# Pacing a weight preparation by the steps of the product beside it, and exchanging two operations between VectorE and GpSimd

## The chip, the cores and the metric

The kernel runs on one core of one Trainium2 chip. The metric is the device time of one execution in microseconds; lower is better. Engines are named as in the profile: PE is TensorE, DVE is VectorE, ACT is ScalarE, POOL is GpSimd and SP is SyncE, whose queue issues nearly all DMAs here.

## The reference

Three stages in float32, one after the other, on 4 x 576 = 2304 tokens of 512 columns:

```
local = softmax(causal(q k^T / 8)) v                 # 4 batches, 8 heads, 64 columns each
mem   = (phi(q) M_prev) / (phi(q) z_prev + 1e-6)     # phi(x) = elu(x) + 1
x     = sigmoid(beta) mem + (1 - sigmoid(beta)) local
r     = relu(x w_in)                                 # 2304 x 2048
y     = (s r^2 + b) w_out                            # 2304 x 512
out   = (sigmoid(y w_gate) * (y w_val)) w_out2       # inner width 1536
```

The weights arrive as 64-bit floats. s and b are one number each.

## The kernel before, in words

Every matrix product is made from split numbers: an operand is rounded to a high part, the low part is the difference, and three products (high x high, low x high, high x low) are summed in PSUM. So every operand costs a rounding on ScalarE and a subtraction on VectorE or GpSimd.

The program runs in overlapping stages. In the attention stage, 16 jobs (a batch and two heads) give x, batch by batch; `s_hi` and `s_lo` (lines 886 to 894) split x into its parts, in two windows of 256 and 320 tokens for each batch. h = x w_in is made in 128 blocks (`h_mm`, line 310) of 12 matmuls each, 16 column blocks for each of 8 windows; ScalarE applies the relu and r goes to DRAM (`h_store`). When attention is over, y is made: 6 windows of 384 tokens times 16 column blocks are 96 steps (`plan_step`, line 1013). One step loads 128 x 384 numbers of r (SyncE), squares them (ScalarE), makes s r^2 + b in place (`scale`, line 1027), rounds them to gh (`g_hi`, ScalarE), makes the low part gl (`g_lo`, line 1038) and multiplies both with w_out in 12 matmuls (`y_mm`). Each buffer is one of a few: 4 for r, 3 each for gh and gl.

Each 64-bit weight tile of 128 x 512 numbers is turned into float32 by integer operations (`weight_parts`): `scaled` on ScalarE, two VectorE passes in `rest` (lines 250 and 253), a third in `joined` (line 259); a split weight then gets its high part (ScalarE) and low part (GpSimd, line 268). w_in has 16 tiles, w_out 16, w_out2 12. w_gate and w_val together are 12 blocks n of two tiles each (`plan_blocks`, line 1129): each block gets four sums on VectorE (line 1159), and the seven 256-column pieces are stored in DRAM (weight_scratch). These raw tiles share 4 buffers with those of w_out.

The last stage takes y in three pairs of windows. For each pair, the products m of y's combinations with the seven pieces are made in 12 groups (gate and value of one column block f in turn, `plan_group`); their sums on VectorE give, after a sigmoid and a multiplication on GpSimd, the rows f and f + 6 of p, which has 12 rows. `plan_out` (line 1361) then makes each of six output tiles of 128 tokens in three thirds of four rows of p each, with w_out2.

The order of the work is not that of the program text. A planner (`Plan.order`) is given tasks with an engine, an estimated duration, a due time ("urgency"), buffers to hold and tasks to follow, simulates the engines, and lets each free engine take the ready task with the lowest due time. Its result is the fixed order of instructions on every engine. `late` is the time that it adds before a task counts as finished (60 ns, 250 for TensorE, 1900 or 2500 for DMAs). The due times come from the table `TUNE`: w_gate and w_val's is `gv` + n x `gvs`, y's is `y` + 10 for each step, h's is `h` + `hs` for each block.

Of the kernel before, what the change touches and what calls it, by code (L numbers as in the profile page):

```python
# [8 lines left out]
F32 = mybir.dt.float32  # L9
# [21 lines left out]
}  # L31
ENG = {"split": "POOL"}
RR = 4
RAW2 = 4
RING = 5
SETS = 3


class Plan:
# [25 lines left out]
    def order(self):  # L65
# [34 lines left out]
        while len(out) < len(tasks):  # L100
            for eng in clock:
                if clock[eng] > now:
                    continue
                for n in ready.get(eng, []):
                    t = tasks[n]
                    if not can(t):
                        continue
                    ready[eng].remove(n)
                    for tag, x in t[6]:
                        free[tag] -= 1  # L110
                        if tag in heads:
                            heads[tag] += 1
                    self.start[n] = now
                    out.append(n)
                    clock[eng] = now + t[1]
                    end = now + t[1] + t[7]
                    if t[8]:
                        dma = max(dma, now + t[1]) + t[8] / RATE
                        end = max(end, dma + t[7])
                    heapq.heappush(events, (end, n))  # L120
                    heapq.heappush(events, (clock[eng], -1))
                    break
            assert events, [
                (tasks[n][3], tasks[n][6]) for q in ready.values() for n in q
            ]
            now = max(now, events[0][0])
            changed = set()
            while events and events[0][0] <= now:
                _, n = heapq.heappop(events)
                if n < 0:  # L130
                    continue
                for x in tasks[n][5]:
                    touches[x] -= 1
                    if not touches[x] and x in self.made:
                        free[self.made[x][0]] += 1
# [12 lines left out]
def attention_moe_kernel(  # L148
# [58 lines left out]

    def load_consts():

        nc.sync.dma_start(gt, beta.partition_broadcast(P))  # L210
        nc.sync.dma_start(sb_s, s_in.partition_broadcast(P))
        nc.sync.dma_start(sb_b, b_in.partition_broadcast(P))
# [211 lines left out]
    def stack_lo(t, ds):  # L424
# [10 lines left out]
        "raw2": RAW2, "f2": FB, "w2": 16, "rr": RR, "gh": 3, "gl": 3, "yacc": 2,  # L435
# [495 lines left out]
    def plan_weight(pool, src, name, cols, u, key, tag, done=None, ins=(), late=False):  # L931

        raw, fl = ("raw2", "f2") if late else ("raw", "f")
        box, load, scaled, rest, joined, high, low = weight_parts(
            pool, src, name, cols, Late("stage") if late else stage
        )
        add(
            "SP", 450, load, u + AT["lw"], reads=ins,
            new=[(raw, ("raw", key))] + ([(tag, key)] if tag else []), late=1900, size=5e5,
        )  # L940
        add("ACT", 670, scaled, u, reads=[("raw", key)], new=[(fl, ("f", key))])
        add("DVE", 1500, rest, u, writes=[("raw", key)])
        add("DVE", 850, joined, u, reads=[("f", key)], writes=[("raw", key)])
        if tag:
            add("ACT", 660, high, u, reads=[("raw", key)], writes=[key])
            add("POOL", 1360, lambda: done(low()), u, reads=[("raw", key)], writes=[key])
        return box
# [65 lines left out]
    def plan_step(step):  # L1013
# [12 lines left out]

        def scale():
            r = r_sb[step]
            nc.vector.tensor_scalar(  # L1029
                out=r, in0=r, scalar1=sb_s, scalar2=sb_b, op0=ALU.mult, op1=ALU.add  # L1030
            )

        def g_hi():
            gh = Y["gp"].tile([P, WT], F32R, tag="gh", name=f"gh{wi}_{f}", bufs=3)
            nc.scalar.copy(gh, r_sb[step])  # L1035
            gs[step] = [gh]

        def g_lo():
            gl = Y["gp"].tile([P, WT], F32R, tag="gl", name=f"gl{wi}_{f}", bufs=3)
            nc.gpsimd.tensor_tensor(  # L1040
                out=gl, in0=r_sb.pop(step), in1=gs[step][0].bitcast(F32), op=ALU.subtract
            )
            gs[step].append(gl)
# [22 lines left out]
            size=n * 512,  # L1066
        )
        add("ACT", act(n), square, v, writes=[rk])
        add("DVE", 450, scale, v, writes=[rk])
        add("ACT", act(n), g_hi, v, reads=[rk], new=[("gh", gk)])  # L1070
        add("POOL", 130 + 2.4 * n, g_lo, v, reads=[rk, gk], new=[("gl", ("gl", step))])
        new = [("yacc", ("ya", wi))] if f == 0 else []
        add(
            "PE", 12 * mm(n), y_mm, u,
# [54 lines left out]
    def plan_blocks(n):  # L1129
# [5 lines left out]
        raws = [  # L1135
            plan_weight(
                None, src[:, (f + i * HF) * P : (f + i * HF + 1) * P], f"gv{n}_{i}", True, u + i,
                keys2[i], None, ins=["bar1"], late=True,
            )
            for i in range(2)  # L1140
        ]
# [22 lines left out]
        add("DVE", 900, lambda: sums(0), u, reads=[k0, k1, ("wm", n)], writes=[("wm", n, 1)])  # L1164
        add("DVE", 900, lambda: sums(1), u, reads=[k0, k1, ("wm", n)], writes=[("wm", n, 1)])
# [89 lines left out]
    def plan_group(pi, g, f, u):  # L1255
# [67 lines left out]
        for i, xs in enumerate(PAIRS):  # L1323
            m, k = len(xs) * 2 * P, ("ws", z, i)
            add("ACT", 130 + 0.9 * m, lambda i=i: hi(i), v + i, reads=[("wf", z)], new=[("ws", k)])
            add(
                LOS[i], 150 + 1.05 * m if LOS[i] == "DVE" else 130 + 2.4 * m, lambda i=i: lo(i),
                v + i, reads=[("wf", z)], writes=[k],
            )
        k = lambda o: ("c", z, o)  # L1330
# [18 lines left out]
        for o in (0, 3, 2, 1):  # L1349
# [8 lines left out]
                writes=[("pp", pi, f + HF * OF[o][0], OF[o][1])], new=new,  # L1358
            )

    def plan_out(pi, tt, u):

        h, r = divmod(tt, WT // P)
# [2 lines left out]

        def hi(i):
            t = Z["ps", z, i] = Y["ws"].tile([P, 2, 512], F32R, tag="ws", name=f"ps{pi}_{tt}_{i}")
            nc.scalar.copy(t[:, 0].rearrange("p (f n) -> p f n", n=P), src(i))  # L1369

        def src(i):
            return Z["p", pi][:, 4 * i : 4 * i + 4, h, r * P : (r + 1) * P]

        def lo(i):
            t = Z["ps", z, i]
            nc.vector.tensor_tensor(  # L1376
                out=t[:, 1].rearrange("p (f n) -> p f n", n=P), in0=src(i),
                in1=t[:, 0].bitcast(F32).rearrange("p (f n) -> p f n", n=P), op=ALU.subtract,
            )

        def out_mm(i):
            if i == 0:
                Z["zo", z] = Y["ps_zo"].tile([P, DM], F32, tag="zo", name=f"o{pi}_{tt}")
            for k in range(4):
                f = 4 * i + k
                for a, x in ((0, 0), (1, 0), (0, 1)):
                    nc.tensor.matmul(  # L1387
                        Z["zo", z], Z["ps", z, i][:, a, k * P : (k + 1) * P],
                        w_out2_sb[f][:, x].rearrange("p c f -> p (c f)"),
                        start=(f == 0 and a == x == 0), stop=(f == NF2 - 1 and x == 1),  # L1390
                    )

        def evict():
# [5 lines left out]

        v = u - AT["pl"]  # L1400
        for i in range(NF2 // 4):
            ins = [("p", pi)] + [("pp", pi, f, h) for f in range(4 * i, 4 * i + 4)]
            k = ("ps", z, i)
            add("ACT", act(512), lambda i=i: hi(i), v + i, reads=ins, new=[("ws", k)])
            add("DVE", dve(512), lambda i=i: lo(i), v + i, reads=ins, writes=[k])
            add(
                "PE", 12 * mm(512), lambda i=i: out_mm(i), u + i,
                reads=[k, "bar3b"] + [("w3", f) for f in range(4 * i, 4 * i + 4)],
                writes=[("zo", z)] if i else [], new=[] if i else [("zo", ("zo", z))], late=250,
            )  # L1410
        add("DVE" if tt % 2 else "ACT", act(512), evict, u, reads=[("zo", z)], new=[("raw", ("os", z))])
# [111 lines left out]
```

## Time and profile before

| what | value |
|---|---|
| median of 3 runs | 1136.14 us (1135.06 to 1143.1) |
| profiled execution | 1142.42 us, its span 1140.6 us |
| mean granted TensorE clock | 0.975 |
| busy | PE 1056.0, DVE 786.0, ACT 647.3, POOL 619.2 us |
| DMA | 145.93 MB, mean 128 GB/s |
| chain that ended last | PE 71%, DVE 15%, DMA 4%, issue 3%, POOL 3%, ACT 3% |

The span is the profiled part of one execution; the time beside it has the start and end around it. "Busy" of an engine counts the time in which it works on an instruction, and for a matmul also some of the time in which it waits inside. The chain is followed back from the last instruction to whatever released each step.

### The profile page before, as it was taken

The numbers are of one execution on the slowest core, as the hardware profiler recorded it, in microseconds if no ns is written. First come the engines' busy times: TensorE is split into PE (matmuls) and PEld (weight loads), VectorE is DVE, ScalarE is ACT, GpSimd is POOL, SyncE is SP. The second block draws the span as 40 slices with busy tenths as digits, with TensorE's granted clock in tenths as the row PEclk, the third lists the DMA queues.
The fourth block names the chain that finished last, engine by engine and source line by source line (L and its number), as shares of the span: only waits on it lengthen the run. The fifth ranks groups of instructions, "written<-read, shape, count | busy, mean of one in ns | idle before, by whom it ended". The sixth has DMA issues, their size and how long they took to land.

```text
span 1140.6 us, 18761 instructions
## 1 busy us (share of the span) xinstructions
PE 1056.0 (93%) x6496; PEld 986.6 (86%) x6496; DVE 786.0 (69%) x1426; ACT 647.3 (57%) x1407; POOL 619.2 (54%) x598
## 2 busy tenths in 40 slices
PE   4776999999999989988789999999799998999998
PEld 3665999899999989988688999998689997899986
DVE  5999888777677527868999433999826667166631
ACT  4877777777777655545656544555425553245421
POOL 5657566744454335733665653999615775157710
PEclk9989899999999999988899999999999999999999
DMA  5333453333232157649588634545114330043100
GB/s 129 76 78 100 120 158 119 85 94 94 83 95 66 59 185 207 197 139 346 184 250 289 218 112 133 205 156 193 59 44 146 130 129 10 37 138 130 66 19 37
DMA packets 135598, 145.93 MB, mean 128 GB/s; under 512 B 68176, under 2 KB 123472, under 8 KB 135504
## 3 DMA queue, kind: packets, MB, share of 16 engines
q1 hardware_dynamic: 135504, 144.74, 40.5%
q8 instruction: 51, 0.84, 0.3%
q14 instruction: 43, 0.35, 0.1%
HBM read 106.96 MB, written 37.75 MB: 127 GB/s over the span
## 4 chain that ended last, share of the span: by engine, by line
PE 71%; DVE 15%; DMA 4%; issue 3%; POOL 3%; ACT 3%; SPq 0%; ACTq 0%; DVEq 0%; POOLq 0%
PE m L1291 19%; PE h L316 15%; PE o L1387 13%; PE y L1054 11%; PE sc L623 3%; PE acc L803 2%; PE acc L804 2%; DMA rr<-relu_scratch 1%; DVE wm L1159 1%; PE pt_B L750 1%; DVE rr L1029 1%; PE sc L649 1%; PE ft L413 1%; POOL p L1313 1%; DVE yt L1190 1%
## 5 line engine op out<-in xcount | busy, mean ns | idle before, releaser
L1291 PE MATMUL m<-yt,ws 128*128 128x384 f32 x1512 | 266.9, 336 | 6.5 <-POOL ws L1275 3.9
L1291 PEld LDWEIGHTS m<-yt,ws 128*128 128x128 f32 x1512 | 263.6, 189 | 9.1 <-POOL ws L1275 4.8
L316 PE MATMUL h<-x,w_in 128*128 128x256 f32 (+1 forms) x1536 | 233.6, 305 | 6.9 <-ACT r L326 6.9
L316 PEld LDWEIGHTS h<-x,w_in 128*128 128x128 f32 x1536 | 214.3, 194 | 13.1 <-ACT r L326 8.2
L1303 DVE TENSOR_TENSOR set<-m,set 128x384 f32<-128x384 f32 x252 | 134.2, 553 | 57.4 <-PE m L1291 55.3
L1275 POOL TENSOR_TENSOR ws<-wf,ws 128x512 fp32r<-128x512 f32 (+1 forms) x108 | 123.8, 1165 | 90.5 <-ACT ws L1267 90.4
L1054 PE MATMUL y<-gh,w_out 128*128 128x384 f32 x768 | 155.9, 344 | 17.8 <-ACT gh L1035 16.4
L1040 POOL TENSOR_TENSOR gl<-rr,gh 128x384 fp32r<-128x384 f32 x96 | 111.2, 1169 | 112.2 <-ACT gh L1035 83.9
L1387 PE MATMUL o<-w_out,ps 128*128 128x512 f32 x648 | 155.6, 401 | 8.8 <-DVE ps L1376 8.8
L1387 PEld LDWEIGHTS o<-w_out,ps 128*128 128x128 f32 x648 | 123.6, 191 | 39.7 <-DVE ps L1376 10.0
L1054 PEld LDWEIGHTS y<-gh,w_out 128*128 128x128 f32 x768 | 137.6, 193 | 22.4 <-ACT gh L1035 18.8
L1267 ACT CAST ws<-wf 128x512 fp32r<-128x512 f32 (+1 forms) x144 | 81.1, 568 | 94.2 <-PE m L1291 66.7
L1029 DVE TENSOR_SCALAR rr<-rr,sb_s,sb_b 128x384 f32<-128x384 f32 x96 | 62.5, 663 | 71.5 <-ACT rr L1025 69.2
L1313 POOL TENSOR_TENSOR p<-set,set 128x384 f32<-128x384 f32 x72 | 85.2, 1206 | 45.4 <-DVE set L1303 45.4
L681 POOL TENSOR_SCALAR P<-P,rs 128x384 f32<-128x384 f32 (+3 forms) x144 | 82.9, 599 | 42.0 <-DVE rs L673 24.2
L603 DVE CUSTOM_DVE_ANT_0 P<-sc,mask 128x384 f32<-128x384 f32 (+2 forms) x144 | 70.8, 515 | 34.7 <-PE sc L623 19.2
L665 ACT ACTIVATE P<-P,nm 128x384 f32<-128x384 f32 (+2 forms) x144 | 83.8, 583 | 7.4 <-DVE nm L603 6.7
L1054 PE MATMUL y<-gl,w_out 128*128 128x384 f32 x384 | 84.4, 341 | 1.1 <-POOL gl L1040 1.1
L326 ACT ACTIVATE r<-h 128x320 f32<-128x320 f32 (+1 forms) x128 | 52.2, 409 | 57.3 <-PE h L316 42.2
L1376 DVE TENSOR_TENSOR ps<-p,ps 128x512 fp32r<-128x512 f32 x54 | 47.1, 886 | 50.6 <-ACT ps L1369 50.2
L1025 ACT ACTIVATE rr<-rr 128x384 f32<-128x384 f32 x96 | 49.4, 524 | 50.9 <-DMA rr<-relu_scratch 48.8
L1054 PEld LDWEIGHTS y<-gl,w_out 128*128 128x128 f32 x384 | 69.5, 192 | 2.3 <-POOL gl L1040 2.3
(134 smaller groups left out, 1709.8 us busy)
## 6 DMA issues: line engine op xcount, KB each, us to landing
wf<-weight_scratch SPq DMA_DIRECT2D x36, 896.0 KB, 4.6
rr<-relu_scratch SPq DMA_DIRECT2D x96, 192.0 KB, 3.3
raw_w_out<-in_moe_w_out_dram SPq DMA_DIRECT2D x28, 512.0 KB, 4.3
weight_scratch<-wm SPq DMA_DIRECT2D x12, 896.0 KB, 8.0
relu_scratch<-r SPq DMA_DIRECT2D x32, 320.0 KB, 2.3
raw_w_in<-in_moe_w_in_dram SPq DMA_DIRECT2D x16, 512.0 KB, 4.1
relu_scratch<-r SPq DMA_DIRECT2D x32, 256.0 KB, 2.5
raw_gv<-in_moe_w_gate_dram SPq DMA_DIRECT2D x12, 512.0 KB, 5.6
```

The costliest lines, as they stand in the source:

```text
L316: nc.tensor.matmul(t[:, :n], wt[:, wi, c], x[:, xi, c], start=(m == 0), stop=(m == 3 * NK - 1))
L665: nc.scalar.activation(pr, pr, AF.Exp, bias=T.pop(("nm", j, e, t)), scale=-1.0, accum_out=T["sums", j][:, col : col + 1],)
L681: nc.gpsimd.tensor_scalar(out=pr, in0=pr, scalar1=T["rs", j, part][:, n : n + 1], scalar2=1.0, op0=ALU.mult, op1=ALU.mult,)
L1029: nc.vector.tensor_scalar(out=r, in0=r, scalar1=sb_s, scalar2=sb_b, op0=ALU.mult, op1=ALU.add)
L1040: nc.gpsimd.tensor_tensor(out=gl, in0=r_sb.pop(step), in1=gs[step][0].bitcast(F32), op=ALU.subtract)
L1054: nc.tensor.matmul(accs[wi][d][:, :n], w_out_sb[f][:, x, d], y, start=(f == 0 and x == 0 and y is gh), stop=(f == NF - 1 and y is gl),)
L1267: nc.scalar.copy(t[:, 0, :m], flat(a, m))
L1275: engine[LOS[i]].tensor_tensor(out=t[:, 1, :m], in0=flat(a, m), in1=t[:, 0, :m].bitcast(F32), op=ALU.subtract)
L1291: nc.tensor.matmul(acc, wt[:, a, k : k + P], yt[:, y, c], start=(m == 0), stop=(m == 3 * K2 - 1),)
L1303: nc.vector.tensor_tensor(out=t[:, o], in0=Z["m", z, x], in1=t[:, i], op=ALU.add)
L1313: engine[TIMES[o]].tensor_tensor(out=p[:, f + HF * OF[o][0], OF[o][1]], in0=Z["set", z][:, o], in1=Z["set", zg][:, o], op=ALU.mult,)
L1387: nc.tensor.matmul(Z["zo", z], Z["ps", z, i][:, a, k * P : (k + 1) * P], w_out2_sb[f][:, x].rearrange("p c f -> p (c f)"), start=(f == 0 a ...
```

## The change

The diff, cut to its core:

```diff
-    "pv": 28.5, "split": 117.6, "h": 9920.5, "hs": 56.8, "w": 297.3, "ws": 26.9, "lw": -287.4,
-    "relu": -5000.0, "wo": 31942.3, "wos": 7.3, "gv": 42719.0, "gvs": 58.2, "y": 16976.0,
-    "lead": 25.8, "lr": -189.7, "ys": -139.5, "yss": 39.3, "t0": 63.0, "z": 59940.3, "zw": 311.1,
+    "pv": 34.9, "split": 71.5, "h": 1670.1, "hs": 50.3, "w": 304.5, "ws": 26.9, "lw": -333.7,
+    "relu": -5000.0, "wo": 29200.4, "wos": -2.6, "gv": 39111.5, "gvs": 110.0, "y": 16143.2,
+    "lead": 12.1, "lr": -288.0, "ys": -104.6, "yss": 53.8, "t0": 4.3, "z": 60013.8, "zw": 410.0,
...
-ENG = {"split": "POOL"}
-RR = 4
+ENG = {"split": "DVE"}
+RR = 6
+GG = 4
...
+PACE = 2, 7
@@ class Plan
-                    heapq.heappush(events, (end, n))
-                    heapq.heappush(events, (clock[eng], -1))
+                    heapq.heappush(events, (end, n, 0))
+                    heapq.heappush(events, (clock[eng], n, 1))
...
                 for m in users[n]:
+                    if (tasks[m][0] == tasks[n][0] and not tasks[n][8]) != bool(same):
+                        continue
                     waiting[m] -= 1
@@ load_consts
-        nc.sync.dma_start(gt, beta.partition_broadcast(P))
+        nc.scalar.dma_start(gt, beta.partition_broadcast(P))
...
@@ plan_weight
-        add("DVE", 1500, rest, u, writes=[("raw", key)])
-        add("DVE", 850, joined, u, reads=[("f", key)], writes=[("raw", key)])
+        add("DVE", 1700, rest, u, writes=[("raw", key)])
+        add("DVE", 950, joined, u, reads=[("f", key)], writes=[("raw", key)])
@@ plan_step
         def scale():
-            nc.vector.tensor_scalar(
+            nc.gpsimd.tensor_scalar(
...
         def g_lo():
-            gl = Y["gp"].tile([P, WT], F32R, tag="gl", name=f"gl{wi}_{f}", bufs=3)
-            nc.gpsimd.tensor_tensor(
+            gl = Y["gp"].tile([P, WT], F32R, tag="gl", name=f"gl{wi}_{f}", bufs=GG)
+            nc.vector.tensor_tensor(
...
-        add("DVE", 450, scale, v, writes=[rk])
+        add("POOL", 700, scale, v, writes=[rk])
...
-        add("POOL", 130 + 2.4 * n, g_lo, v, reads=[rk, gk], new=[("gl", ("gl", step))])
+        add("DVE", 650, g_lo, v, reads=[rk, gk], new=[("gl", ("gl", step))])
@@ plan_blocks
-                keys2[i], None, ins=["bar1"], late=True,
+                keys2[i], None, ins=["bar1", ("yc", PACE[0] + PACE[1] * n)], late=True,
...
@@ plan_out
+    THIRD = [list(range(4)), list(range(HF, HF + 4)), [HF - 2, HF - 1, NF2 - 2, NF2 - 1]]
...
-            ins = [("p", pi)] + [("pp", pi, f, h) for f in range(4 * i, 4 * i + 4)]
+            ins = [("p", pi)] + [("pp", pi, f, h) for f in THIRD[i]]
```

In words:

- The raw loads of block n of w_gate and w_val may be planned only after step 2 + 7n of y.
- s r^2 + b moves from VectorE to GpSimd, the low part of g from GpSimd to VectorE. There are 6 buffers for r instead of 4, and 4 each for gh and gl instead of 3. The low part of x (`s_lo`) moves from GpSimd to VectorE.
- In the planner, a task that follows one on its own engine is ready when the engine is free; `late` holds for followers on other engines and for all followers of DMAs.
- The output's thirds are rows 0 to 3, rows 6 to 9, and rows 4, 5, 10, 11 of p, instead of 0 to 3, 4 to 7 and 8 to 11. High and low parts are taken by the same rows.
- The three loads of constants are issued by ScalarE instead of SyncE.
- The due times in `TUNE` have new values (the first, second and last lines of the table are left out above), and some planned durations of VectorE are longer (weights, sums, weight splits).

## Rows read from the trace of the kernel before

**Rows 1.** Busy time by stage: length, then PE, PEld, DVE, ACT, POOL, clock, DMA.
```profile
0.00:120.00 120.00, 81.89 (x506) 65.67 (x507) 98.47 (x234) 81.90 (x194) 75.93 (x97) 0.92 0.39 96
120.00:405.00 285.00, 283.36 (x2276) 270.57 (x2276) 207.66 (x511) 214.16 (x533) 144.42 (x182) 1.00 0.33 95
405.00:500.00 95.00, 87.64 (x573) 85.07 (x571) 60.93 (x77) 51.29 (x109) 53.40 (x37) 0.98 0.67 209
500.00:620.00 120.00, 101.51 (x520) 97.60 (x521) 108.64 (x159) 68.75 (x140) 58.92 (x45) 0.90 0.74 246
620.00:705.00 85.00, 85.00 (x490) 84.76 (x488) 34.23 (x50) 41.31 (x88) 45.15 (x43) 1.00 0.49 154
705.00:810.00 105.00, 93.05 (x506) 89.08 (x505) 99.59 (x136) 59.45 (x114) 91.94 (x69) 0.98 0.51 172
```
**Rows 2.** PE in order of time: start, duration, instructions of y and h.
```profile
450.61 1.55 PE L1054 MATMUL y<-gh,w_out 128*128 128x384 f32 x8
...
452.69 1.91 PE L316 MATMUL h<-x,w_in 128*128 128x320 f32 x12
454.44 1.55 PE L1054 MATMUL y<-gh,w_out 128*128 128x384 f32 x8
```
**Rows 3.** Waits of PE, 405 to 705 us: total, times, longest.
```profile
PE y L1054 <- ACT gh L1035: 16.4, 7, 5.0
PE h L316 <- ACT r L326: 6.9, 3, 3.3
```
**Rows 4.** DVE in order of time: passes with nothing on POOL beside them.
```profile
520.61 0.42 DVE L1159 TENSOR_TENSOR wm<-raw_gv 128x256 f32<-128x256 f32 x1
...
522.08 0.42 DVE L250 TENSOR_SCALAR raw_gv<-raw_gv 128x512 int32<-128x512 int32 x1
522.53 0.69 DVE L253 SCALAR_TENSOR_TENSOR raw_gv<-raw_gv 128x512 int32<-128x512 int32 x1
523.33 0.69 DVE L259 SCALAR_TENSOR_TENSOR raw_gv<-f_gv,raw_gv 128x512 int32<-128x512 int32 x1
...
635.83 0.69 DVE L1275 TENSOR_TENSOR ws<-wf,ws 128x512 fp32r<-128x512 f32 x1 [2.25 <-ACT ws L1267]
```
**Rows 5.** DVE by line, 500 to 620 us; the last row 705 to 810.
```profile
L253 DVE SCALAR_TENSOR_TENSOR raw_gv<-raw_gv 128x512 int32<-128x512 int32 x21 | 20.5, 975 | 0.7
L259 DVE SCALAR_TENSOR_TENSOR raw_gv<-f_gv,raw_gv 128x512 int32<-128x512 int32 x21 | 19.0, 905 | 1.3
L250 DVE TENSOR_SCALAR raw_gv<-raw_gv 128x512 int32<-128x512 int32 x22 | 16.8, 763 | 1.5 <-DMA raw_gv<-in_moe_w_gate_dram 1.5
...
L253 DVE SCALAR_TENSOR_TENSOR raw_w_out<-raw_w_out 128x512 int32<-128x512 int32 x12 | 16.8, 1402 | 0.4
```
**Rows 6.** The two lines that change engine: ns least/median/most, whole span.
```profile
L1029 DVE TENSOR_SCALAR rr<-rr,sb_s,sb_b x96: 467/480/1974, 416.4 to 694.8; 128x384 f32<-128x384 f32 x96
L1040 POOL TENSOR_TENSOR gl<-rr,gh x96: 999/1122/3030, 417.7 to 699.0; 128x384 fp32r<-128x384 f32 x96
```
**Rows 7.** POOL by line and shape, whole span: count, busy us, mean ns.
```profile
L681 POOL TENSOR_SCALAR P<-P,rs 128x384 f32<-128x384 f32 x32 | 19.5, 613 | 42.0 <-DVE rs L673 24.2 <-DVE rs L677 9.0 <-PE acc L807 8.8
```
**Rows 8.** POOL and DVE in order of time at 103 us.
```profile
103.30 2.38 POOL L892 TENSOR_TENSOR x<-XB,x 128x1024 fp32r<-128x1024 f32 x1 [2.00 <-ACT x L888]
103.44 2.79 DVE L253 SCALAR_TENSOR_TENSOR raw_w_in<-raw_w_in 128x512 int32<-128x512 int32 x1
```
**Rows 9.** POOL in order of time: the last split of x.
```profile
409.73 2.96 POOL L892 TENSOR_TENSOR x<-XB,x 128x1280 fp32r<-128x1280 f32 x1 [2.54 <-ACT x L888]
```
**Rows 10.** SP's queue at the start.
```profile
0.74 0.39 SPq L210 DMA_DIRECT2D gt<-in_beta_dram  x1
...
2.12 0.98 SPq L373 DMA_DIRECT2D rawk<-in_k_dram  x2
```
**Rows 11.** PE in order of time where the output starts, with the wait.
```profile
810.48 2.08 PE L1387 MATMUL o<-w_out,ps 128*128 128x512 f32 x4 [4.23 <-DVE ps L1376]
...
952.69 3.66 PE L1387 MATMUL o<-w_out,ps 128*128 128x512 f32 x9 [2.87 <-DVE ps L1376]
```

More of the change, by code (lines that the diff above doesn't have):

```diff
@@ L128, in order @@
             while events and events[0][0] <= now:
[L129 to L135, printed above, removed]
+                _, n, same = heapq.heappop(events)
+                if not same:
+                    for x in tasks[n][5]:
+                        touches[x] -= 1
+                        if not touches[x] and x in self.made:
+                            free[self.made[x][0]] += 1
                 for m in users[n]:
+                    if (tasks[m][0] == tasks[n][0] and not tasks[n][8]) != bool(same):
+                        continue
                     waiting[m] -= 1
@@ L208, in load_consts @@
     def load_consts():
-        nc.sync.dma_start(gt, beta.partition_broadcast(P))
-        nc.sync.dma_start(sb_s, s_in.partition_broadcast(P))
-        nc.sync.dma_start(sb_b, b_in.partition_broadcast(P))
+        nc.scalar.dma_start(gt, beta.partition_broadcast(P))
+        nc.scalar.dma_start(sb_s, s_in.partition_broadcast(P))
+        nc.scalar.dma_start(sb_b, b_in.partition_broadcast(P))
         nc.scalar.activation(gt, gt, AF.Exp, scale=-1.0)
@@ L434, in attention_moe_kernel @@
         "PTC": 1, "XB": 1, "x0": 1, f"x{SPLIT}": 1, "raw": 2, "f": FB, "wt": 16,
-        "raw2": RAW2, "f2": FB, "w2": 16, "rr": RR, "gh": 3, "gl": 3, "yacc": 2,
+        "raw2": RAW2, "f2": FB, "w2": 16, "rr": RR, "gh": GG, "gl": GG, "yacc": 2,
         "yf": 2, "wf": 2, "ws": RING, "set": SETS, "p": 1, "w3": NF2, "z": 4, "zz": 2,
@@ L1033, in g_hi @@
         def g_hi():
-            gh = Y["gp"].tile([P, WT], F32R, tag="gh", name=f"gh{wi}_{f}", bufs=3)
+            gh = Y["gp"].tile([P, WT], F32R, tag="gh", name=f"gh{wi}_{f}", bufs=GG)
             nc.scalar.copy(gh, r_sb[step])
@@ L1163, in plan_blocks @@
         add("ACT", 360, lambda: copies(1), u, reads=[k1, ("wm", n)], writes=[("wm", n, 0)])
-        add("DVE", 900, lambda: sums(0), u, reads=[k0, k1, ("wm", n)], writes=[("wm", n, 1)])
-        add("DVE", 900, lambda: sums(1), u, reads=[k0, k1, ("wm", n)], writes=[("wm", n, 1)])
+        add("DVE", 1100, lambda: sums(0), u, reads=[k0, k1, ("wm", n)], writes=[("wm", n, 1)])
+        add("DVE", 1100, lambda: sums(1), u, reads=[k0, k1, ("wm", n)], writes=[("wm", n, 1)])
         add(
@@ L1326, in plan_group @@
             add(
-                LOS[i], 150 + 1.05 * m if LOS[i] == "DVE" else 130 + 2.4 * m, lambda i=i: lo(i),
+                LOS[i], 150 + 1.75 * m if LOS[i] == "DVE" else 130 + 2.4 * m, lambda i=i: lo(i),
                 v + i, reads=[("wf", z)], writes=[k],
@@ L1368, in hi, with part @@
             t = Z["ps", z, i] = Y["ws"].tile([P, 2, 512], F32R, tag="ws", name=f"ps{pi}_{tt}_{i}")
-            nc.scalar.copy(t[:, 0].rearrange("p (f n) -> p f n", n=P), src(i))
+            nc.scalar.copy(part(t, 0, i), src(i))
+        def part(t, x, i):
+            return t[:, x].rearrange("p (a f n) -> p a f n", a=1 + i // 2, n=P)
         def src(i):
-            return Z["p", pi][:, 4 * i : 4 * i + 4, h, r * P : (r + 1) * P]
+            p = Z["p", pi][:, :, h, r * P : (r + 1) * P]
+            if i < 2:
+                return p[:, i * HF : i * HF + 4].unsqueeze(1)
+            return p.rearrange("p (a f) n -> p a f n", a=2)[:, :, 4:]
         def lo(i):
@@ L1376, in lo @@
             nc.vector.tensor_tensor(
-                out=t[:, 1].rearrange("p (f n) -> p f n", n=P), in0=src(i),
-                in1=t[:, 0].bitcast(F32).rearrange("p (f n) -> p f n", n=P), op=ALU.subtract,
+                out=part(t, 1, i), in0=src(i), in1=part(t, 0, i).bitcast(F32), op=ALU.subtract,
             )
@@ L1384, in out_mm @@
             for k in range(4):
-                f = 4 * i + k
+                f = THIRD[i][k]
                 for a, x in ((0, 0), (1, 0), (0, 1)):
@@ L1389, in out_mm @@
                         w_out2_sb[f][:, x].rearrange("p c f -> p (c f)"),
-                        start=(f == 0 and a == x == 0), stop=(f == NF2 - 1 and x == 1),
+                        start=(i == k == a == x == 0), stop=(i == 2 and k == 3 and x == 1),
                     )
@@ L1407, in plan_out @@
                 "PE", 12 * mm(512), lambda i=i: out_mm(i), u + i,
-                reads=[k, "bar3b"] + [("w3", f) for f in range(4 * i, 4 * i + 4)],
+                reads=[k, "bar3b"] + [("w3", f) for f in THIRD[i]],
                 writes=[("zo", z)] if i else [], new=[] if i else [("zo", ("zo", z))], late=250,
```

6 rows, old and new, of the table TUNE are left out of this document.

## Prediction

> **What bounds the kernel now.** I read the busy time by stage first [rows 1]. From 120 to 405 us TensorE is busy 283.4 of 285 us; nothing on another engine can shorten that stage. Before 120 us it has 38 us idle, and VectorE is the full engine there (98.5 of 120). From 405 to 705 us the 16 remaining blocks of h for the last batch, all of y and the preparation of w_out, w_gate and w_val run together. In its middle, 500 to 620, VectorE is busy 108.6 of 120 us and TensorE's granted clock falls to a mean of 0.90; in the last 85 us TensorE is busy all the time and VectorE only 34.2. The work is the same in kind and badly spread.
>
> How much is lost in these 300 us? The three stages hold 1583 matmuls [rows 1], 1152 of them y's (96 steps of 12). The timeline gives a step of y as 452.69 - 450.61 = 2.08 us and a block of h on 320 columns as 454.44 - 452.69 = 1.75 us [rows 2]. So y needs 96 x 2.08 = 200 us. The other 431 matmuls are h on 320 columns (0.146 us each), h on 256 (scaled, 0.117) and 24 of the products m (as y's, 0.173); at a mean of about 0.135 us they need 58. Together 258 of 300 us: **42 us are lost**. The waits of TensorE name 16.4 us in seven waits of y for the high part gh on ScalarE and 6.9 us of h for ScalarE's r [rows 3]; the rest is matmuls at the reduced granted clock (the 0.90 of that stage) and short waits. ScalarE is only the messenger: gh waits for s r^2 + b on VectorE, and VectorE works through w_gate and w_val meanwhile.
>
> **The change, part by part.**
>
> *Pacing.* Twelve blocks, each two raw tiles and four sums on VectorE, are now due after steps 2, 9, ..., 79 of y instead of whenever a buffer is free. Undisturbed, one raw tile costs VectorE 0.42 + 0.69 + 0.69 = 1.80 us and one sum 0.42 [rows 4]: a block is 2 x 1.80 + 4 x 0.42 = 5.28 us. In the crowded stage the three passes took 0.763 + 0.975 + 0.905 = 2.64 us [rows 5], a factor of 1.47, so a block there cost about 7.8 us. 21 of the 24 raw tiles were worked on in these 120 us [rows 5]. Spread, one falls on seven steps, 7 x 2.08 = 14.56 us. The wait on y is in the plan alone; in the program it is a place in SyncE's queue and in VectorE's order, behind the loads of r, so no instruction gets a new semaphore. What queues behind a late weight load on SyncE is a load of r; six r and four g buffers are ahead of it, about four steps or 8 us of cover. The last block is begun at step 79, 17 steps or 35 us before y ends, and its group is the last of the first pass over m; nothing waits for it.
>
> *The swap of engines.* s r^2 + b (VectorE, 0.48 us median) goes to GpSimd; the low part (GpSimd, 1.12 us median) goes to VectorE [rows 6]. On GpSimd a one-input operation on 128x384 took 0.613 us [rows 7]; on VectorE a two-input one takes 0.42 us on 256 columns and 0.69 on 512 [rows 4], so 0.555 on 384. GpSimd falls from 1.12 to 0.61 us a step, VectorE rises from 0.48 to 0.555 undisturbed. The bounds of the low part are 0.555 us and, at the factor 1402/690 = 2.03 that the worst stage shows for a two-input pass [rows 5, 4], 1.13.
>
> Does VectorE fit into 14.56 us? Seven low parts and a block are 7 x 0.555 + 5.28 = 9.17 us undisturbed; y's evictions (12 x 0.55) and the six passes of the first transform (768 columns, 0.96 by the same slope) add 12.4 us over 96 steps, 0.9 per seven. At the factor 1.47 all of it is 14.6: just full. At 1.0 it is 10.1. I take a value between, near 1.3 (13 us), since GpSimd's operation is half as long and its share of a step falls from 1.12/2.08 to 0.61/2.08.
>
> That disturbance is plain in one pair: a GpSimd subtraction from 103.30 to 105.68 us, and a VectorE pass of nominally 0.69 us from 103.44 to 106.23 [rows 8]. The Trainium skill, SBUF — State Buffer, section "Who interferes with whom", says that a VectorE instruction with two SBUF inputs and a GpSimd one that reads SBUF exclude each other for the whole instruction, the later one waiting. This pair agrees (2.79 us = the rest of GpSimd's plus one pass). By the rule alone the delay would be the rest of a 0.61 us operation met 3 times in 10, some 0.1 us for each of 17 passes: 11.7 us in 14.56, and the forecast 4 us lower than mine. The rule also speaks against the swap, since it puts a second two-input operation on VectorE.
>
> *Order on TensorE.* In the planner a successor on the same engine is now ready when the engine is free, not 60 or 250 ns later, and h's due time falls from 9920 to 1670. Blocks of h no longer have a planned pause into which a step of y slips (before: y and h in turn [rows 2]). TensorE's work is the same. With h in one piece, two r buffers must be stored in about 3.5 us instead of 7.5, against the opening burst of loads (six r, four w_out): the wait of h for ScalarE's r (6.9 us [rows 3]) stays, and I leave 7 us for it.
>
> So the stretch keeps 7 us at its opening plus 3 us of small waits, between 5 and 25: **42 becomes 10, -32 us.**
>
> *x's low part on VectorE.* The last one held GpSimd 2.96 us with nothing beside it for h to use [rows 9]; on VectorE 1280 columns cost about 1.5 by the slope: -1.5 us there. The other seven lie in VectorE's full first stage or beside TensorE's full second: 8 us of VectorE gained as work, the blocking of rows 8 saved; nil, between -3 and +3.
>
> *Constants on ScalarE's queue.* SyncE issued three small loads from 0.74 us and the first K at 2.12 [rows 10]; the first transpose waited for that K. -1.4 us; ScalarE has nothing to do by then but its table load.
>
> *Output columns by readiness.* Two transitions to the output wait for the low part of p, 4.23 and 2.87 us [rows 11]. The last third still needs the last group, so the wait is shortened by what the second third can fill: -2 us, between 0 and -7.
>
> *Due times and VectorE's planned durations.* No row shows them. In the first 120 us they move loads and order on a full VectorE; in 705 to 810 VectorE is full too (99.6 of 105 [rows 1]) with the second w_out. I take 0, between -10 and +10.
>
> Sum: -32 - 1.5 - 1.4 - 2 = -37. The profiled execution took 1142.4 us: 1105.5. The median of the runs shown is 1136.1, 6.3 lower, so **1099 us**.
>
> **The rivals.**
>
> *VectorE stays just full* (factor 1.47, passes in the wrong order in front of low parts). For it: the low part is now the last link before TensorE and stands in the queue that has the weights. Half of the 42 us stays: -16 - 5 = -21, 1115.
>
> *Slower: the low part on VectorE becomes the bound of y.* At the factor 2.03 the seven steps need 9.17 x 2.03 + 1.5 = 20.1 us of VectorE, 5.5 over TensorE's 14.56 in each of 12 blocks: 66 + 7 us lost instead of 42, less 5 elsewhere: +26, 1162. It decides from 17.9 us per seven steps on (12 x 3.3 + 7 = 42 + 5). Against it: that factor was measured with GpSimd busy 92 of 105 us [rows 1]; here it has 0.61 in 2.08.
>
> *The change doesn't do what it says.* The pacing is a due time; if GpSimd and DMA delays let VectorE's static order bunch the blocks as before, only the small terms are left: 1131. Against it: SyncE's loads of r, held by buffers that y frees, stand between the weight loads.
>
> *More than forecast.* The first 120 us gain 10 by order as well, and y's stretch loses 6 us instead of 10: 1085.
>
> **How the numbers follow.** The forecast (1099, its own range 1088 to 1112) has 0.58, half the gain 0.20, the slower case 0.08, no spread 0.07, more gain 0.07. The range holds all but the slower case and half of the no-spread one, widened by the 10 us either way of the due times: 1078 to 1132. A measurement of this kernel tells about 1% (11 us) from no change. Faster by over 1% (below 1125) takes the forecast, nearly all of half the gain and the last: 0.80, with a little off for the due times; within 1% 0.11; slower 0.09.
>
> **What would show it.** Right: from h's end to y's end TensorE runs steps every 2.08 us at full clock, the waits of y for gh are nearly gone, VectorE is evenly at 75 to 90% there, the first products m start near 668 us instead of 705.9, and the stage after it keeps its length. The low part's mean on VectorE is 0.6 to 0.85 us, GpSimd's scale 0.6 to 0.75. Wrong: a mean of the low part over 1.0 us with TensorE waiting for it; h broken by waits for r's store for more than 10 us; or a first stage that ends later than 120 us.

## The result, and the profile after

The changed kernel takes 1091.0 us (median of 4 runs, 1090.1 to 1093.2) against 1137.3 for the kernel before (4 runs): a ratio of 0.9588, 95% interval 0.9548 to 0.9629. That ratio makes 47 us; the two medians differ by 46. The forecast was 37 us less, 1099 us, within 1078 to 1132. The profiled execution takes 1091.8 us (span 1090.0), 50.6 less than that of before.

Busy time by stage, columns as in [rows 1]; the borders follow the stages of this kernel:

```profile
0.00:120.00 120.00, 89.60 (x557) 74.62 (x558) 99.79 (x239) 85.06 (x199) 73.23 (x97) 0.83 0.40 101
120.00:400.00 280.00, 275.25 (x2210) 261.56 (x2208) 206.64 (x512) 212.49 (x525) 137.02 (x174) 1.00 0.33 95
400.00:500.00 100.00, 97.04 (x649) 96.03 (x649) 65.91 (x95) 59.92 (x127) 49.98 (x41) 1.00 0.72 233
500.00:620.00 120.00, 119.00 (x687) 118.67 (x686) 95.93 (x155) 76.41 (x160) 75.47 (x61) 1.00 0.72 238
620.00:662.00 42.00, 42.00 (x244) 42.00 (x243) 23.06 (x41) 22.08 (x48) 18.16 (x18) 1.00 0.73 251
662.00:767.00 105.00, 98.22 (x537) 93.47 (x536) 97.70 (x139) 61.37 (x115) 92.50 (x70) 0.99 0.50 172
```

From 500 to 620 us TensorE is busy 119.0 of 120 us with 687 matmuls at the full granted clock, where it had 520 at 0.90; VectorE falls from 108.6 to 95.9 us while it serves more steps. The last stage of the table is as tight as before: VectorE 97.7 and GpSimd 92.5 of 105 us.

TensorE's waits from 400 to 662 us (total, times, longest) answer to [rows 3]:

```profile
PE h L319 <- ACT r L329: 1.6, 2, 0.8
PE y L1057 <- ACT gh L1038: 1.0, 1, 1.0
PE y L1057 <- POOL w_out L271: 0.8, 1, 0.8
PE y L1057 <- ACT w_out L268: 0.6, 1, 0.6
```

16.4 us of waits for gh have become 1.0, and h's 6.9 for r 1.6. After h's end every step of y follows the last by 2.08 us, but for two at the one wait for gh (3.25 and 2.22 us at 546 us) (TensorE in order of time, as [rows 2]):

```profile
461.76 1.19 PE L319 MATMUL h<-x,w_in 128*128 128x320 f32 x7
462.79 1.55 PE L1057 MATMUL y<-gh,w_out 128*128 128x384 f32 x8
464.18 0.85 PE L1057 MATMUL y<-gl,w_out 128*128 128x384 f32 x4
464.87 1.55 PE L1057 MATMUL y<-gh,w_out 128*128 128x384 f32 x8
```

VectorE by line from 500 to 620 us, as [rows 5], and the two lines that changed engine over the whole span (ns least/median/most), as [rows 6]:

```profile
L1043 DVE TENSOR_TENSOR gl<-rr,gh 128x384 fp32r<-128x384 f32 x57 | 42.5, 753 | 19.4 <-ACT gh L1038 12.4 <-PE y L1057 6.4
L256 DVE SCALAR_TENSOR_TENSOR raw_gv<-raw_gv 128x512 int32<-128x512 int32 x17 | 13.9, 818 | 0.6
L262 DVE SCALAR_TENSOR_TENSOR raw_gv<-f_gv,raw_gv 128x512 int32<-128x512 int32 x16 | 10.9, 682 | 0.0
L253 DVE TENSOR_SCALAR raw_gv<-raw_gv 128x512 int32<-128x512 int32 x17 | 7.8, 457 | 1.9 <-DMA raw_gv<-in_moe_w_val_dram 1.9
...
L1032 POOL TENSOR_SCALAR rr<-rr,sb_s,sb_b x96: 661/1089/2665, 413.1 to 648.3; 128x384 f32<-128x384 f32 x96
L1043 DVE TENSOR_TENSOR gl<-rr,gh x96: 543/559/2207, 414.4 to 653.6; 128x384 fp32r<-128x384 f32 x96
```

A raw tile now costs VectorE 0.457 + 0.818 + 0.682 = 1.96 us instead of 2.64 (means). The price moved to GpSimd: s r^2 + b takes 1.09 us in the median, where 0.66 is the least.

Where the 50.6 us are, by milestones of the profiled executions of all kernels that follow (us; the last matmul of attention, the starts of the last matmul of y and of the long runs of output matmuls in the chain of waits). A name with u_ is the changed kernel with one part undone, with d_ the kernel before with a part done. "Ratio" is that of all timed runs to the kernel before, measured beside it. d_pace has no milestones, because its profiled execution took 3540 us where its other nine took 1138 to 1149.

| kernel | ratio, 95% interval | attention ends | from there to y's end | to the first output's end | to the third output's start | rest of span |
|---|---|---|---|---|---|---|
| before | 1 | 402.4 | 302.3 | 151.9 | 229.8 | 54.1 |
| changed | 0.9588 (0.9548 to 0.9629) | 400.0 | 261.5 | 149.2 | 225.1 | 54.2 |
| u_pace | 0.9596 (0.9560 to 0.9632) | 399.4 | 262.0 | 147.5 | 225.1 | 54.2 |
| u_third | 0.9609 (0.9559 to 0.9658) | 399.6 | 261.6 | 147.9 | 226.1 | 54.7 |
| u_slow | 0.9632 (0.9596 to 0.9668) | 402.4 | 267.1 | 148.4 | 225.2 | 54.5 |
| u_tune | 0.9657 (0.9626 to 0.9688) | 403.5 | 264.5 | 152.9 | 225.1 | 54.4 |
| u_swap | 0.9662 (0.9624 to 0.9701) | 396.4 | 270.4 | 148.4 | 225.1 | 54.2 |
| u_dur | 0.9697 (0.9664 to 0.9730) | 404.6 | 267.7 | 155.3 | 225.2 | 54.2 |
| u_buf | 0.9702 (0.9671 to 0.9732) | 397.4 | 273.1 | 149.3 | 225.1 | 54.2 |
| u_plan | 0.9836 (0.9801 to 0.9871) | 402.8 | 289.8 | 143.6 | 233.2 | 51.5 |
| d_plan_swap | 0.9875 (0.9846 to 0.9905) | 398.8 | 288.1 | 157.1 | 226.0 | 54.2 |
| d_swap | 0.9910 (0.9880 to 0.9941) | 401.4 | 288.7 | 151.8 | 229.8 | 54.1 |
| d_plan | 1.0031 (1.0011 to 1.0051) | 400.1 | 304.7 | 157.8 | 226.0 | 54.2 |
| d_pace | 1.0041 (1.0016 to 1.0067) | | | | | |

40.8 of the 50.6 us lie between the end of attention and the end of y. Of these, 4.2 are 24 products m that the kernel before slipped in ahead of y's end (24 x 0.173), so the next column, which gains 2.7, gained 6.9 on equal work. The work in this column differs in other rows too: u_plan and d_swap also have these 24 products in it, and after the end of attention u_tune has 12 matmuls of h more to do than the 420 of most rows, u_plan 24 more, u_dur, d_plan and d_plan_swap 36 more (about 0.146 us each). In u_plan 12 output matmuls come behind six products m, so its last three columns are cut at other points; their sum, 428.3 us, is that of the changed kernel (428.5). The attention column differs by 5 us between kernels whose difference lies behind it (397.4 to 402.4 for u_buf and u_slow); its -2.4 can't be told from that.

The ratios of the table are good to some 6 us when two rows are compared (from their intervals), so a difference of 5 us needs the milestones beside it.

### The profile page after: what moved, and what is told of

It reads as the page before. It is cut to its first block, busy times and chain, and to the rows that moved or that the text cites. A ratio compares the mean times of both kernels' runs of the same rounds, so it can differ in the third digit from the quotient of the medians.

```text
span 1090.0 us, 18804 instructions
## 1 busy us (share of the span) xinstructions
PE 1040.3 (95%) x6496; PEld 977.0 (90%) x6496; DVE 766.3 (70%) x1434; ACT 647.6 (59%) x1407; POOL 598.4 (55%) x590
## 4 chain that ended last, share of the span: by engine, by line
PE 80%; DVE 7%; POOL 7%; issue 2%; ACT 2%; DMA 1%; SPq 0%; DVEq 0%; POOLq 0%; ACTq 0%
PE m L1294 17%; PE h L319 17%; PE y L1057 16%; PE o L1397 14%; PE sc L626 3%; PE acc L806 3%; PE acc L807 2%; DVE set L1306 2%; PE pt_B L753 1%; PE sc L652 1%; POOL ws L1278 1%; POOL p L1316 1%; PE acc L810 1%; POOL w_out L271 1%; POOL P L684 1%
## 5 line engine op out<-in xcount | busy, mean ns | idle before, releaser
L1294 PE MATMUL m<-yt,ws 128*128 128x384 f32 x1512 | 264.5, 335 | 4.9 <-POOL ws L1278 3.5
L1294 PEld LDWEIGHTS m<-yt,ws 128*128 128x128 f32 x1512 | 262.0, 188 | 7.2 <-POOL ws L1278 4.7
L319 PE MATMUL h<-x,w_in 128*128 128x256 f32 (+1 forms) x1536 | 224.6, 300 | 5.5 <-POOL w_in L271 2.0
L319 PEld LDWEIGHTS h<-x,w_in 128*128 128x128 f32 x1536 | 207.8, 189 | 11.5 <-issue 3.7
L1032 POOL TENSOR_SCALAR rr<-rr,sb_s,sb_b 128x384 f32<-128x384 f32 x96 | 103.8, 1088 | 96.7 <-ACT rr L1028 92.9
L1057 PE MATMUL y<-gh,w_out 128*128 128x384 f32 x768 | 149.1, 335 | 2.4 <-ACT gh L1038 1.0
L1057 PEld LDWEIGHTS y<-gh,w_out 128*128 128x128 f32 x768 | 134.3, 188 | 3.3 <-ACT gh L1038 1.3
L1043 DVE TENSOR_TENSOR gl<-rr,gh 128x384 fp32r<-128x384 f32 x96 | 66.9, 701 | 51.5 <-PE y L1057 24.0
L606 DVE CUSTOM_DVE_ANT_0 P<-sc,mask 128x384 f32<-128x384 f32 (+2 forms) x144 | 70.5, 516 | 29.4 <-PE sc L626 13.6
L1057 PE MATMUL y<-gl,w_out 128*128 128x384 f32 x384 | 82.0, 334 | 0.0
L1374 ACT CAST ps<-p 128x512 fp32r<-128x512 f32 x54 | 32.5, 620 | 64.1 <-PE o L1397 50.6
L1038 ACT CAST gh<-rr 128x384 fp32r<-128x384 f32 x96 | 48.8, 511 | 33.2 <-PE y L1057 26.0
```

Of the source, the lines that this page charges most:

```text
L319: nc.tensor.matmul(t[:, :n], wt[:, wi, c], x[:, xi, c], start=(m == 0), stop=(m == 3 * NK - 1))
L606: nc.vector.tensor_tensor_reduce(out=pr, in0=ps, in1=mk, scale=1.0, scalar=3e38, op0=ALU.add, op1=ALU.min, accum_out=nm,)
L1032: nc.gpsimd.tensor_scalar(out=r, in0=r, scalar1=sb_s, scalar2=sb_b, op0=ALU.mult, op1=ALU.add)
L1057: nc.tensor.matmul(accs[wi][d][:, :n], w_out_sb[f][:, x, d], y, start=(f == 0 and x == 0 and y is gh), stop=(f == NF - 1 and y is gl),)
L1294: nc.tensor.matmul(acc, wt[:, a, k : k + P], yt[:, y, c], start=(m == 0), stop=(m == 3 * K2 - 1),)
```

## Experiments

My theory was the prediction's: the pacing spreads VectorE's weight work, and the stalls of y vanish with it. The rivals were the exchange of engines, the planner's rule (order), and the output's thirds for the transitions.

**u_pace**, the pacing undone:

```diff
-                keys2[i], None, ins=["bar1", ("yc", PACE[0] + PACE[1] * n)], late=True,
+                keys2[i], None, ins=["bar1"], late=True,
```

> The changed kernel with the pacing alone taken out (blocks of w_gate and w_val planned as soon as their buffers are free). Pacing theory: the blocks bunch again, VectorE is full for some 100 us and TensorE waits in y for gh; 20 to 30 of the 40 us gained between the end of attention and the end of y come back, 1111 to 1121 us. Swap theory (the exchange of engines alone made room on VectorE): under 5 us come back, at most 1096.

1092.3 us, y's stretch 262.0 against 261.5: nothing comes back, so the pacing as such is worth nothing in this kernel. The last loads of w_val are issued 25 us earlier without the pacing (SyncE's queue in order of time, changed kernel, then u_pace):

```profile
631.21 0.56 SPq L233 DMA_DIRECT2D raw_gv<-in_moe_w_val_dram  x1
```
```profile
606.60 1.07 SPq L233 DMA_DIRECT2D raw_gv<-in_moe_w_val_dram  x2
```

and y is as dense. But the run takes away little of the spread. VectorE works through a fixed order, so one can count how many of y's 96 steps it has served when it begins a raw tile of w_gate or w_val: the first and last of the 24 tiles stand after 12 and 88 steps in the changed kernel, after 12 and 81 in u_pace, and after 20 and 60 in the kernel before. Other parts of the change keep the blocks apart without the pacing; which of them stays open. (The due times of the blocks lie behind those of y in the kernel before too, where the blocks bunch.) What the spread itself is worth is seen in d_pace below.

**u_swap**, the exchange undone:

```diff
-            nc.gpsimd.tensor_scalar(
+            nc.vector.tensor_scalar(
...
-            nc.vector.tensor_tensor(
+            nc.gpsimd.tensor_tensor(
```

> The changed kernel with s r^2 + b back on VectorE and the low part back on GpSimd, with the planned durations of before; all else as changed. Pacing theory: seven steps and a block still fit (about 13.9 us of VectorE at the factor 1.47 against 14.56), so 0 to 8 us come back, 1091 to 1099. Swap theory: 20 us and more come back, 1111 or above, with VectorE's weight passes slowed by GpSimd's 1.1 us subtractions as before.

1100.7 us, y's stretch +8.9: just above the pacing theory's bound and far from the swap theory's. VectorE by line, 500 to 620 us, and GpSimd's low part:

```profile
L1032 DVE TENSOR_SCALAR rr<-rr,sb_s,sb_b 128x384 f32<-128x384 f32 x53 | 38.1, 745 | 6.3 <-ACT rr L1028 6.3
L262 DVE SCALAR_TENSOR_TENSOR raw_gv<-f_gv,raw_gv 128x512 int32<-128x512 int32 x16 | 18.3, 1145 | 1.1
L256 DVE SCALAR_TENSOR_TENSOR raw_gv<-raw_gv 128x512 int32<-128x512 int32 x16 | 15.2, 952 | 0.5
L253 DVE TENSOR_SCALAR raw_gv<-raw_gv 128x512 int32<-128x512 int32 x16 | 11.3, 709 | 3.8 <-DMA raw_gv<-in_moe_w_val_dram 3.5 <-DMA raw_gv<-in_moe_w_gate_dram 0.2
...
L1043 POOL TENSOR_TENSOR gl<-rr,gh 128x384 fp32r<-128x384 f32 x54 | 64.4, 1203 | 43.7 <-ACT gh L1038 29.7 <-PE y L1057 4.4 <-DVE rr L1032 2.8
```

What VectorE itself does for a step costs the same either way (0.745 or 0.753 us). VectorE pays on the other lines: a raw tile is back at 2.81 us. But what TensorE waits for in y is GpSimd's low part, 5.5 us in two waits. The long one stands behind two operations of y's first transform on GpSimd (all engines in order of time):

```profile
539.12 1.55 PE L1057 MATMUL y<-gh,w_out 128*128 128x384 f32 x8
539.95 2.46 POOL L1198 TENSOR_TENSOR yf<-yf,yf 128x768 f32<-128x768 f32 x1 [2.37 <-DVE yf L1198]
542.37 1.93 POOL L1193 TENSOR_TENSOR yt<-yf,yt 128x768 fp32r<-128x768 f32 x1
...
545.49 1.65 PE L1057 MATMUL y<-gl,w_out 128*128 128x384 f32 x4 [4.81 <-POOL gl L1043]
```

After it TensorE's granted clock is 0.50 from 545 to 550 us, the lower of its two levels, so this one stall and the slow matmuls behind it are about 7 of the 8.9 us. That VectorE's slower tiles cost y time in this run is not shown.

**u_plan**, the planner's old rule, and **d_plan**, the new rule alone:

```diff
-                    if (tasks[m][0] == tasks[n][0] and not tasks[n][8]) != bool(same):
+                    if same:
                         continue
```

> The changed kernel with the planner's old rule (a follower on the same engine waits for the added 60 or 250 ns too). Order theory (the gain comes from TensorE's and VectorE's order being planned without those pauses): 15 us or more come back, 1106 or above. Pacing theory: the order of y against the weights is set by the pacing, so at most 8 come back, 1091 to 1099.

1119.5 us: +28 us of y's stretch, the largest effect of all. Of these, 4.2 are the 24 products m that are in it again and 3.5 are 24 matmuls of h that attention left over; about 21 are lost time. In this kernel the plan counts 2.39 us for a step of y that takes 2.08. Here is one of the stalls (all engines in order of time):

```profile
624.62 7.41 SPq L1025 DMA_DIRECT2D rr<-relu_scratch  x3
...
627.51 0.68 ACT L250 ACTIVATE f_gv<-raw_gv 128x512 f32<-128x512 f32 x1 [3.25 <-DMA raw_gv<-in_moe_w_val_dram]
627.51 0.43 DVE L253 TENSOR_SCALAR raw_gv<-raw_gv 128x512 int32<-128x512 int32 x1 [2.91 <-DMA raw_gv<-in_moe_w_val_dram]
...
628.08 0.51 ACT L1038 CAST gh<-rr 128x384 fp32r<-128x384 f32 x1
...
628.64 2.50 PE L1057 MATMUL y<-gh,w_out 128*128 128x384 f32 x8 [2.12 <-ACT gh L1038]
```

ScalarE and VectorE both stand, in their fixed order, before a weight tile that has not landed, while the gh that TensorE needs is queued behind; TensorE then runs its next eight matmuls in 2.50 us instead of 1.55 (its granted clock is 0.70 from 628 to 631 us). VectorE's waits for such loads from 460 to 690 us sum to 15.7 us here and 1.9 in the changed kernel. This is a wait that the prediction had called covered: what queues behind a late weight load has "about four steps or 8 us of cover". The loads of r are late as well: in u_plan they make up 6.3% of the chain that ended last, in no other kernel of the table more than 2.2%.

> The kernel before with the planner's new rule alone (old due times, engines, buffers). Order theory: undoing the rule cost 27 us, so done alone it gains 15 to 30, about 1107 to 1122; steps of y and blocks of h no longer alternate. Pacing theory: weights still bunch, so under 10 us, 1127 or above.

1143.0 us, no gain: order alone is not it either. Most of h is now in two long runs (72 and 156 matmuls; its last one starts at 498.6 instead of 506.5 us). The waits have only changed place: those of h for r (6.9 us [rows 3]) are gone, and y waits instead, from 396 to 706 us:

```profile
PE y L1055 <- ACT gh L1036: 19.9, 9, 6.3
PE y L1055 <- ACT r L327: 5.9, 1, 5.9
```

One column shows the rule by itself: to the third output's start, 229.8 us before and 226.0 with the rule alone.

**u_slow**, the new rule kept, a step of y planned 250 ns longer:

```diff
-            "PE", 12 * mm(n), y_mm, u,
+            "PE", 12 * mm(n) + 250, y_mm, u,
```

> The changed kernel, new rule kept, with a step of y planned 250 ns longer (2.39 us; it takes 2.08 on the chip). Plan theory: this alone makes TensorE overtake the other engines' fixed order in y; most of the 27 us that the old rule cost come back, 1104 to 1119, with the weight blocks about 16.7 us apart. Interleaving theory (the old rule cost because steps of y slip between blocks of h): 0 to 5 us, at most 1096.

1097.7 us; between the two expectations, and its interval touches that of the changed kernel. y's stretch is 5.6 us longer, with 10.5 us of VectorE's waits for weight loads. The longest stall, before 602.9 us, follows such a wait of 1.3 us and one of ScalarE for a load of r of 3.6. So the wrong length of y's step by itself costs a fifth of u_plan's 28 us, and VectorE's waits for weight loads need not cost y anything: u_dur below has 9.6 us of them and no wait of y for gh. The rest of the rule acts on every chain of tasks on one engine, and which of them matters stays open.

**u_third**, the old thirds of the output:

```diff
-    THIRD = [list(range(4)), list(range(HF, HF + 4)), [HF - 2, HF - 1, NF2 - 2, NF2 - 1]]
+    THIRD = [list(range(4)), list(range(4, 8)), list(range(8, 12))]
```

> The changed kernel with the output's thirds in the old order of columns. My prediction gave this part 2 us: 1093. If the two transitions to the output that got shorter between the traces (by about 7 and 5 us) owe it to the order of the columns, 8 to 12 come back: 1099 to 1103, with waits of the output for VectorE's low part of p of 3 to 4 us at the first and the second transition.

1092.1 us: 1.0 us comes back at the second transition (226.1 against 225.1; all seven kernels of the table with the new thirds and the new rule lie at 225.1 or 225.2), none at the first. The chain of waits shows the second output starting without a break in the changed kernel and after a break of 8.5 us with few matmuls in u_third (start, length, matmuls in one run; changed kernel, then u_third):

```profile
810.66 87.36 PE m L1294 x504
898.03 50.39 PE o L1397 x216
```
```profile
809.09 85.32 PE m L1294 x492
902.95 44.83 PE o L1395 x191
```

Most of that break is the same work counted in other pieces (12 products and 25 output matmuls, 2.1 + 5.8 us); the third column gives the real difference.

**d_pace**, the pacing alone on the kernel before (the edit of u_pace the other way round):

> The kernel before with the pacing alone (a block planned after every seventh step of y). Pacing theory as predicted: 15 to 30 us gained, 1107 to 1122. Order theory: the plan still counts 2.39 us for a step that takes 2.08, so TensorE overtakes VectorE's fixed order with or without the pacing; 0 to 12 us gained, 1125 to 1137.

1143.4 us: no gain, and this run decides against the pacing. The order of VectorE's instructions doesn't depend on the times of an execution, and there the 24 raw tiles stand after 20 to 86 of y's 96 steps, against 20 to 60 in the kernel before. The blocks were spread over two thirds more steps, and nothing was won: my theory falls here. Whether bunched blocks would cost time in the changed kernel no run shows, since none bunches them there.

**d_swap**, the exchange alone:

> The kernel before with the exchange of engines alone (s r^2 + b on GpSimd, low part on VectorE). Undoing it cost about 8 us; alone 4 to 12 gained, 1125 to 1133. Swap theory (VectorE's slowed passes are the cause of the stalls): 20 or more, 1117 or below.

1129.8 us, a gain of about 10 us as expected, 13.6 us of it in y's stretch; the only one of the three parts done alone that gains anything.

**d_plan_swap**, rule and exchange:

> The kernel before with the planner's new rule and the exchange of engines, no pacing, old due times and buffers. If these two carry the change: 30 to 42 us gained, 1095 to 1107. If the new due times and buffers are needed for it: no better than the rule alone, 1112 to 1122.

1125.0 us, above both expectations and hardly better than the exchange alone. The waits of y for gh are still there, in a kernel with the old buffers, due times and planned durations:

```profile
PE y L1055 <- ACT gh L1036: 12.8, 8, 4.3
```

The next three runs take up that remainder.

**u_buf**, 4 buffers of r and 3 of gh and gl:

```diff
-RR = 6
-GG = 4
+RR = 4
+GG = 3
```

> The changed kernel with 4 buffers of r and 3 of gh and gl, as before. Buffer theory (the six and four buffers are the cover that keeps TensorE from waiting for VectorE): the waits of y for gh come back, 8 to 15 us, 1099 to 1106. If the order of the plan is what matters: 0 to 4 us, at most 1095.

1104.6 us, as the buffer theory expected. y's stretch is 11.6 us longer, with the waits back (396 to 671 us):

```profile
PE y L1057 <- ACT gh L1038: 6.4, 7, 3.3
PE y L1057 <- DVE gl L1043: 2.1, 2, 1.5
```

What the buffers cover is mostly GpSimd and not VectorE, as the theory had it: in the same stretch ScalarE waits with gh for GpSimd's s r^2 + b 20.2 us in 25 waits, against 6.1 in 7 in the changed kernel (396 to 662 us).

**u_dur**, VectorE's old planned durations:

```diff
-        add("DVE", 1700, rest, u, writes=[("raw", key)])
-        add("DVE", 950, joined, u, reads=[("f", key)], writes=[("raw", key)])
+        add("DVE", 1500, rest, u, writes=[("raw", key)])
+        add("DVE", 850, joined, u, reads=[("f", key)], writes=[("raw", key)])
```

> The changed kernel with VectorE's old planned durations (weight passes 1500 and 850 ns instead of 1700 and 950, sums 900 instead of 1100, weight splits 1.05 ns a column instead of 1.75); nothing else of the program's work. Plan theory (the fixed order must not promise more than VectorE delivers): 8 to 15 us come back with waits of y for gh, 1099 to 1106. Otherwise 0 to 4 us.

1103.9 us: the size as expected, the place not. There are no waits of y for gh at all. Attention ends 4.6 us later with 456 instead of 420 matmuls of h still to do (36 more, about 5 us, in the stretch's +6.2), and the products after y take 6.1 us longer, where w_out2 is prepared. So the durations matter where VectorE is the full engine: after y, and by this trace at the start (4.6 and 5 us together are twice the scatter noted above, but the profiled execution is the slowest of its four by 4 us).

**u_tune**, the old due times:

> The changed kernel with the old table of due times. From the runs so far: rule and exchange with the old table gave 1125, so if the table is what is missing, 15 to 30 us come back, 1106 to 1121, part of it between the end of y and the first output (+5). If buffers, pacing and durations are what is missing, 2 to 8 us, 1093 to 1099. By my prediction, which put the due times at nil: no change.

1101.2 us, between its two expectations: about 8 us come back, 3.5, 3.0 (1.8 of them 12 matmuls of h) and 3.7 in the first three columns, so also the guess "part of it before the first output" holds. The attention part is within the scatter noted above.

## Why the prediction was right or wrong

**What bounds it: right.** 42 us were lost between the end of attention and the end of y. In the longest of y's seven waits for gh, VectorE's weight passes stand in front of s r^2 + b, as I said (the kernel before, all engines in order of time):

```profile
561.43 2.02 DVE L250 TENSOR_SCALAR raw_gv<-raw_gv 128x512 int32<-128x512 int32 x1
...
564.29 0.69 DVE L259 SCALAR_TENSOR_TENSOR raw_gv<-f_gv,raw_gv 128x512 int32<-128x512 int32 x1
564.90 0.86 DVE L1029 TENSOR_SCALAR rr<-rr,sb_s,sb_b 128x384 f32<-128x384 f32 x2
...
565.77 0.91 ACT L1035 CAST gh<-rr 128x384 fp32r<-128x384 f32 x2
...
566.32 2.93 PE L1054 MATMUL y<-gh,w_out 128*128 128x384 f32 x8 [5.03 <-ACT gh L1035]
```

VectorE hardly waits for weight loads there (1.5 us from 460 to 690 us), so these stalls are of another kind than u_plan's. One slip: not 16 blocks of h are left when attention ends but 35 (420 matmuls); the sum counted them rightly. In the changed kernel y takes 96 x 2.08 = 200 us, 420 matmuls of h take 56 (192 x 0.117 + 228 x 0.146), and 262 pass: 6 are lost. I left 10. The first products m start at 661.7 us (forecast 668), but VectorE is not evenly at 75 to 90%: it is busy 66, 80 and 55% of the three stages.

**The pacing: wrong, and it was the step that carried the sum.** "42 becomes 10, -32 us" came true (36.6 on equal work), but u_pace and d_pace give the pacing nothing, with and without the rest. I took the bunching of the blocks, one per ten us, for the cause of the stalls; d_pace spreads the blocks and keeps the time. Waits of y come back when the rule, the buffers or the exchange is undone. The rival that the change doesn't do what it says was priced at 1131 for a kernel without the spread; no run measured such a kernel, since u_pace keeps most of the spread.

**The exchange: direction right, accounts wrong.** I predicted 13 us of VectorE for seven steps and a block; measured are 7 x 0.753 + 2 x 1.96 + 2.02 (sums), which with the 0.9 that I had for evictions and transform makes 12.1 of 14.56. (At the factor 1.47 my own terms give 14.8 and not 14.6, so slightly more than full.) The low part was within 0.6 to 0.85 us (0.70 over the span). GpSimd's operation was not within 0.6 to 0.75: the 0.613 us that I took for it is of attention's normalisation [rows 7], with other work beside it. Of the 96 operations, 68 begin while VectorE is in a two-input operation, and these take 1.24 us on the mean; the other 28 take 0.71. The Trainium skill, SBUF — State Buffer, section "Who interferes with whom", says that a VectorE instruction with two SBUF inputs and a GpSimd one that reads SBUF exclude each other, and that the one issued later waits for the whole of the other. These means agree. The sum of 11.7 us by that rule, which I set beside mine, was nearer than my 13. GpSimd has 1.09 us in a step of 2.08, so little waits for this operation: ScalarE 6.1 us in seven waits, TensorE never (400 to 662 us). In u_swap what comes back is mainly TensorE's wait for a low part on GpSimd, a rival that I had not named: the last link before TensorE stood in GpSimd's queue behind the transform.

**Planner's rule: its cost of zero was wrong.** I put "TensorE's work is the same" and stopped there. Undone it costs 28 us. In the stall shown, gh is queued behind a weight tile whose load is late, which I had called covered. A plan that makes a step of y slower than the chip accounts for about 5 of the 28 us (u_slow); the rest is open.

**Buffers: used as cover in the argument, not priced.** Undone they cost 13 us of the whole, with y's waits for gh back ((0.9702 - 0.9588) x 1137).

**Due times and planned durations: nil, between -10 and +10.** The bound was one for both. They are worth about 8 and 12 us when undone singly, all a gain and together more than the bound.

**Transitions: -2 us became about -12** (6.9 before the first output, 4.7 before the third), but not by the thirds, which gave 1.0. The rule gives 3.8 in the second; due times and durations cost 3.7 and 6.1 in the first when undone.

**Start and x's low part: right as far as they can be seen.** K's load is the first on SyncE's queue (against [rows 10]), and the last low part of x takes 1.49 us on VectorE instead of 2.96 [rows 9]:

```profile
0.74 1.00 SPq L376 DMA_DIRECT2D rawk<-in_k_dram  x2
```
```profile
407.17 1.49 DVE L895 TENSOR_TENSOR x<-XB,x 128x1280 fp32r<-128x1280 f32 x1 [5.64 <-ACT x L891]
```

So the total was near for a wrong reason: the spare time that I gave to one part needed several parts at once. Undone one by one, rule, buffers, durations, exchange and due times cost 28 + 13 + 12 + 8 + 8 = 69 us, of a change that gains 47, each good to some 6 us; of the three done alone, only the exchange gains, about 10. So the parts need each other. How, the traces show for the buffers and the exchange (y waits for gh, or for the low part), and for the durations only where (at the start and after y); for most of the rule and for the due times it stays open.

## What to carry to other kernels

Where a planner fixes the order, a stall shown behind one engine is not priced by moving that engine's work in time: ask first what the plan believes of each duration, the one of the bound engine included, and how many buffers cover the error. When a change has many parts, undo each and do each alone before crediting the one with the best story. And of two engines that exclude each other on memory, give the operation that may wait to the engine for which little waits.

## What was not expected of the hardware

GpSimd's one-input operation on 128x384 took 0.66 us at least and 1.09 in the median beside VectorE's two-input operations, a price that VectorE had paid before (0.682 now against 0.905 for its last weight pass [rows 5]). The waiting hardly became less; the side that bears it changed. An estimate, from the means less the least of the lines of y's steps and of w_gate and w_val's three passes (whole trace): VectorE 39 us before and 19 now, GpSimd 16 and 41.
